# Sliding-window attention and gMLP, four layers: the window mask moved from extra contraction rows to a multiply, and the 64-row remainder of the input projections run as pairs of half-height array tiles

## The chip, the core and the metric

The kernel runs on one core of a Trainium2 chip. The metric is the device time of one execution in microseconds. Three runs of the kernel before took 1401.13, 1403.95 and 1405.71 us; the median is 1403.95 us.

The engines are named as the profile names them: PE is the matrix engine, PEld its weight loads, DVE the vector engine, ACT the scalar engine, POOL the GpSimd engine, and SP the engine that issues most DMAs. SPq, ACTq and POOLq are their DMA queues.

## The reference

The input x has 2048 rows of 576 columns. Four layers run in the order A, B, A, B, and each adds its result to x. Both A layers use the same weights, and so do both B layers.

```
A:  xn = layernorm(x);  q, k, v = xn @ wqkv            (32 heads of 18 columns)
    logits[s, w] = q[s] . k[s - 2w] / sqrt(18),  w = 0..7   (-1e9 where s - 2w < 0)
    x = x + (softmax(logits) @ v) @ wo
B:  xn = layernorm(x);  z = gelu(xn @ w_in)             (576 -> 4608 = 2 x 2304)
    z1 = z[:, :2304];  z2 = layernorm(z[:, 2304:])
    g  = w_sp @ z2 + b_sp                               (w_sp is 2048 x 2048)
    x  = x + (z1 * g) @ w_out
```

A query sees eight keys: its own position and every second one before it.

## The kernel before

All contractions over the 576 columns use the transposed, normalised input `xnT`, a tile of 128 partitions by 5 chunks by 2064 columns. Four chunks are full; the fifth holds 64 columns of x and 64 rows of zeros, which come from zeroed columns 576 to 639 of the LayerNorm output buffers `ln_xn` (four of them, in rotation). A LayerNorm tile is normalised on ACT or POOL (L229, L233) and moved into `xnT` by a transposing DMA on the SP queue (L238).

**Layer A.** `PG` (L469) projects q and k for groups of seven heads and 512 positions: five matmuls of 512 columns into PSUM, then a copy to a staging tile `stg` (L475 on DVE, L477 on ACT, in turn), and, once a staging tile is complete, one DMA for each head into the tile `QK`, where a head has 18 of 32 partitions. Twelve such groups form the prologue, the others are spread over the attention steps. `VW` (L427) makes v. Then come 38 steps, two for each of 19 tiles of 112 queries. In step s, `L_mm` (L546) computes 16 heads' logits as 16 matmuls of 32 rows, four of them in the four row groups of the array; `EXP` (L562 in the late steps, in two halves; L565 in the early ones) takes the exponent on ACT into one of two buffers `P_sb`; `PV` (L588) multiplies by v into the one PSUM tile `O_ps`; `NORM` (L605, L606, on DVE) divides by the sum. A few steps later `TAIL_B` projects with wo (L630), adds x (L632, DVE), and takes LayerNorm statistics for the next layer (L211, DVE), and `TAIL_B2` normalises on POOL (L233). Late steps, which have no `PG` left, carry two dummy matmuls each (L574).

The window is enforced inside `L_mm`: partitions 18 to 31 of each head hold 14 extra rows, for q and for k, whose product is zero inside the window and a large negative number outside it. `build_window_rows` (L120 to L173) makes one period of these rows with small POOL and DVE operations in layer 0 and sends it to DRAM; `fill_window_rows` copies them into `QK`, 16 DMAs of about 225 KB on the SP queue, once in each A layer:

```
        for j in range(4):
            for a in range(2):
                self.dma(QK[32 * j + DH:32 * j + 32, a, :, x0:x1],
                         self.winD[a, :, None, x0:x1].to_broadcast([MR, 8, x1 - x0]), eng=self.nc.sync)
```

In layer 0 these DMAs are issued in the middle of the LayerNorm transposes, in layer 2 at the layer's start.

**Layer B, phase 1** (`p1_main`, 16 row tiles): 2304 columns of z2 as five units (four of 512 columns, one of 256), five matmuls for each (L859); gelu on ACT (L863); sums of squares on DVE (L866) and ACT; a reciprocal root on POOL (L882); the normalised z2 is written by DVE (L895, six slices) and POOL (L892, three slices). Two buffers `zp` hold the gelu output.

**Layer B, phase 2:** 18 times, 20 matmuls of 512 columns for z1 (L943: four column blocks, five chunks) and 64 matmuls for the spatial product (L951). ACT applies gelu (L946), DVE combines (L955, L956). **Phase 3** projects with w_out (L988).

The tile framework orders each engine's instructions by priority. `L_mm` has a raised priority; the rest of a step follows the order of emission.

Of the kernel before, what the change touches and what calls it, by code (L numbers as in the profile page):

```python
# [10 lines left out]
ACT = mybir.ActivationFunctionType  # L11
# [8 lines left out]
P = 128  # L20
# [9 lines left out]
MR = 32 - DH  # L30
WB = 1024.0
# [32 lines left out]
class K:  # L64
# [24 lines left out]
    def setup(self):  # L89
# [10 lines left out]
        nc.vector.memset(self.eps_t[:], EPS)  # L100
        self.xnT = c.tile([P, 5, cfg.XW], bf16, name="xnT")
        nc.gpsimd.memset(self.xnT[:, :, 0:PADL], 0.0)

        self.late_setup = []
# [11 lines left out]
        for b in self.xn_bufs:  # L116
            nc.gpsimd.memset(b[:, D:640], 0.0)
        self.deferred = []

    def build_window_rows(self):  # L120

        nc, c = self.nc, self.consts
        R = c.tile([P, 2, MR, 16], bf16, name="win_rows")
        n = c.tile([P, 3], i32, name="win_n")
        g = c.tile([P, 3], i32, name="win_g")  # L130
        bits = c.tile([P, 5, 3], i32, name="win_bits")
        vf = c.tile([P, 5, 3], f32, name="win_vf")
        uu = c.tile([P, 4, 2], f32, name="win_uu")
        two = c.tile([1, PADL], bf16, name="win_two")
        half = WB / 2
        nc.gpsimd.iota(n[:], pattern=[[1, 3]], base=15, channel_multiplier=1)
        nc.gpsimd.memset(R[:, 0, 0:8, :], half)
        nc.gpsimd.affine_select(out=R[:, 0, 0:8, :], in_=R[:, 0, 0:8, :], compare_op=ALU.is_ge, fill=-half,
                                base=1, pattern=[[2, 8], [-1, 16]], channel_multiplier=0)
        nc.gpsimd.memset(R[:, 1, 0:8, :], 0.0)  # L140
        for off in (2, 3):
            nc.gpsimd.affine_select(out=R[:, 1, 0:8, :], in_=R[:, 1, 0:8, :], compare_op=ALU.not_equal, fill=-1.0,
                                    base=-off, pattern=[[-2, 8], [1, 16]], channel_multiplier=0)
        nc.gpsimd.memset(R[:, 1, 7, 0:2], 1.0)
        for a, v in ((0, half), (1, 1.0)):
            row = R[:, a, 12, :].rearrange("p (f e) -> p f e", e=2)
            nc.gpsimd.memset(row[:, :, 0:1], v)
            nc.gpsimd.memset(row[:, :, 1:2], -v)
        nc.gpsimd.memset(R[:, 0, 13, :], -2.5 * WB)
        nc.gpsimd.memset(R[:, 1, 13, :], 1.0)  # L150
        nc.gpsimd.memset(two[:], 2.0)
        nc.vector.tensor_scalar(out=n[:], in0=n[:], scalar1=15, scalar2=None, op0=ALU.bitwise_and)
        nc.vector.tensor_scalar(out=g[:], in0=n[:], scalar1=1, scalar2=None, op0=ALU.logical_shift_right)
        nc.vector.tensor_tensor(out=g[:], in0=g[:], in1=n[:], op=ALU.bitwise_xor)
        for i in range(4):
            nc.vector.tensor_scalar(out=bits[:, i, :], in0=g[:], scalar1=i, scalar2=1,
                                    op0=ALU.logical_shift_right, op1=ALU.bitwise_and)
        nc.vector.tensor_scalar(out=bits[:, 4, :], in0=n[:], scalar1=1, scalar2=None, op0=ALU.bitwise_and)
        nc.vector.tensor_scalar(out=vf[:], in0=bits[:], scalar1=-2.0, scalar2=1.0, op0=ALU.mult, op1=ALU.add)
        nc.vector.tensor_scalar_mul(out=R[:, :, 0:8, :], in0=R[:, :, 0:8, :], scalar1=vf[:, 4, 1:2])  # L160
        nc.vector.tensor_tensor(out=uu[:], in0=vf[:, 0:4, 0:2], in1=vf[:, 0:4, 1:3], op=ALU.add)
        nc.vector.tensor_scalar_mul(out=R[:, 0, 8:12, :], in0=vf[:, 0:4, 1:2].to_broadcast([P, 4, 16]), scalar1=half)
        nc.vector.tensor_scalar_mul(out=R[:, 1, 8:12, 0:2], in0=uu[:, :, 0:1].to_broadcast([P, 4, 2]), scalar1=0.5)
        nc.vector.tensor_scalar_mul(out=R[:, 1, 8:12, 2:16], in0=uu[:, :, 1:2].to_broadcast([P, 4, 14]), scalar1=0.5)
        one = self.dram.tile([2 * MR, 256], bf16, name="win_period")
        self.winD = self.dram.tile([2, MR, self.cfg.XW], bf16, name="win_all")
        wd = self.winD[:].rearrange("a r x -> (a r) x")
        self.dma(one[:].rearrange("q (p f) -> p q f", f=16), R[0:16].rearrange("p a r f -> p (a r) f"), eng=nc.gpsimd)
        S = self.cfg.S
        self.dma(wd[:, 0:S].rearrange("q (k y) -> q k y", y=256), one[:, None, :].to_broadcast([2 * MR, S // 256, 256]),  # L170
                 eng=nc.gpsimd)
        self.dma(wd[:, S:S + PADL], one[:, 0:PADL], eng=nc.gpsimd)
        self.dma(wd[2 * MR - 1:2 * MR, 0:PADL], two[:], eng=nc.gpsimd)  # L173

    def fill_window_rows(self, QK, x0, x1):
        for j in range(4):
            for a in range(2):
                self.dma(QK[32 * j + DH:32 * j + 32, a, :, x0:x1],
                         self.winD[a, :, None, x0:x1].to_broadcast([MR, 8, x1 - x0]), eng=self.nc.sync)

# [43 lines left out]
    def ln_xn(self, x_t, nrows, mv, rstd, nmr, eng="act"):  # L224
        nc = self.nc
        xn = self.xn_bufs[self.xn_rr % len(self.xn_bufs)]
        self.xn_rr += 1
        if eng == "act":
            nc.scalar.activation(out=xn[:nrows, 0:D], in_=x_t[:nrows, :], func=ACT.Identity,  # L229
                                 scale=rstd[:nrows, 0:1], bias=nmr[:nrows, 0:1])  # L230
        else:
            e = nc.gpsimd if eng == "pool" else nc.vector
            e.tensor_scalar(out=xn[:nrows, 0:D], in0=x_t[:nrows, :], scalar1=mv[:nrows, 0:1],  # L233
                            scalar2=rstd[:nrows, 0:1], op0=ALU.subtract, op1=ALU.mult)
        return xn
# [72 lines left out]
    def layer_A(self, li):  # L308
# [63 lines left out]
        def pad_setup():  # L372
            nc.gpsimd.memset(QK[:, :, :, 0:PADL], 0.0)
            if li == 0:
                self.build_window_rows()
            xc = PADL + CBS[0][1]
            self.fill_window_rows(QK, 0, xc)
            self.fill_window_rows(QK, xc, XW)
# [41 lines left out]
        def VW(t, hh):  # L420
            def f():
# [9 lines left out]
                if hh == 0:  # L431
                    nc.vector.tensor_copy(out=dst, in_=src)
                else:
                    nc.scalar.copy(out=dst, in_=src)
# [14 lines left out]
        def PG(d, qk, cc, use_L=False, in_steps=False):  # L449
            def f():  # L450
# [22 lines left out]
                use_dve = (self.evac_rr % 2 == 0)  # L473
# [63 lines left out]
        def L_mm(s):  # L537
# [5 lines left out]
            for (ftl, j) in order:  # L543
# [3 lines left out]
                                 lhsT=kT[32 * j:32 * j + 32, g, QT * t:QT * t + nk],  # L547
                                 rhs=qT[32 * j:32 * j + 32, g, QT * t + PADL:QT * t + PADL + nq],
# [19 lines left out]
        def JUNK(n):  # L568
# [7 lines left out]
            return f  # L576

# [188 lines left out]
        for s in range(NSTEP):  # L766
            with pr(cfg.prio2):
                EXP(s)
            if s + 1 < NSTEP:
                with pr(cfg.prio):  # L770
                    L_mm(s + 1)
# [23 lines left out]
    def layer_B(self, li):  # L795
# [19 lines left out]
        nc.vector.memset(win2b[64:128, 4 - NPF, :].bitcast(i32), 0)  # L815
        for c in range(NPF, 5):
            kc = 128 if c < 4 else 64
            self.dma(win2b[:kc, c - NPF, :], self.B_w_in[c * P:c * P + kc, Fh:2 * Fh], eng=(nc.sync, nc.scalar)[c % 2])

# [17 lines left out]
        def p1_main(i):  # L837
# [16 lines left out]
            if i == 0:  # L854
                order = [(u, c) for c in range(NPF) for u in units] + [(u, c) for u in units for c in range(NPF, 5)]
            else:
                order = [(u, c) for u in units for c in range(5)]
            for ((ci, c0, sub, w), c) in order:
                nc.tensor.matmul(pzvs[ci][:, sub * 512:sub * 512 + w], lhsT=self.xnT[:, c, PADL + i * P:PADL + (i + 1) * P],  # L859
                                 rhs=win2(c)[:, c0 + sub * 512:c0 + sub * 512 + w],  # L860
                                 start=(c == 0), stop=(c == 4))
# [66 lines left out]
        for jj in range(NB):  # L928
            w1 = p2.tile([P, 5, 256], bf16, name="w1")
            nc.gpsimd.memset(w1[64:128, 4, :], 0.0)  # L930
# [5 lines left out]
            for sub in range(2):  # L936
                z1T = p2.tile([P, S], bf16, name="z1T")
                for q2 in range(0, NQ, 2):
                    nq2 = min(2, NQ - q2)
                    pz1 = self.H_tile("pz1")  # L940
                    for qq in range(nq2):
                        for c in range(5):
                            nc.tensor.matmul(pz1[:, qq, :], lhsT=w1[:, c, sub * P:(sub + 1) * P],  # L943
                                             rhs=self.xnT[:, c, PADL + (q2 + qq) * 512:PADL + (q2 + qq + 1) * 512],
                                             start=(c == 0), stop=(c == 4))
                    nc.scalar.activation(out=z1T[:, q2 * 512:(q2 + nq2) * 512],  # L946
                                         in_=pz1[:, 0:nq2, :].rearrange("p a b -> p (a b)"), func=ACT.Gelu_apprx_tanh)
# [154 lines left out]
```

## Time and profile before

| | |
|---|---|
| profiled execution | 1403.95 us |
| its span | 1401.9 us |
| PE busy | 1251.2 us (89%) |
| DVE busy | 575.4 us (41%) |
| ACT busy | 369.3 us (26%) |
| POOL busy | 343.8 us (25%) |

The profile covers the span from the first instruction to the last; the execution's own time is 2.05 us longer. In the timeline, layer 0 fills the first 220 us or so, layer 1 runs to about 725 us, layer 2 to about 905 us, and layer 3 to the end. Busy shares are averages over all of these; each stage has to be read by itself.

### The profile page before, as it was taken

The page shows a single profiled execution, that of the slowest core. Times are in us where ns is not written, and L with a number is a line of the kernel's source. Part 1 is how long each engine was busy: PE and PEld are TensorE (multiplying, and loading weights), DVE is VectorE, ACT ScalarE, POOL GpSimd, SP SyncE. Part 2 cuts the span into 40 slices and gives each one's busy share as a digit, 9 for nine tenths or more (in the row PEclk, how much of TensorE's full clock was granted, in tenths as well). Part 3 has the DMA queues.
Part 4 walks back from the last instruction along what each step waited for, and adds up shares of the span by engine and source line. Part 5 has one row for each costly group of instructions (what it writes and reads, how often), then busy time and mean ns, then how long its engine had stood idle before and what let it go on. Part 6 is the DMA issues. An engine that isn't in the chain of part 4 may idle for free.

```text
span 1401.9 us, 21432 instructions
## 1 busy us (share of the span) xinstructions
PE 1251.2 (89%) x8656; PEld 659.7 (47%) x8656; DVE 575.4 (41%) x1378; ACT 369.3 (26%) x557; POOL 343.8 (25%) x495
## 2 busy tenths in 40 slices
PE   1089997998999999998994799799999999999997
PEld 0045663443444444444762356444444444444475
DVE  4035674883332332332541367578533332332221
ACT  2045562661111111110221567276310101111000
POOL 7043554881000000001231154568400000000011
PEclk9999999999999999998998899999999999999999
DMA  8954757802000000005759476691200000000132
GB/s 235 111 100 101 139 129 159 165 10 82 9 9 10 9 9 9 1 0 187 192 136 118 98 163 152 143 207 36 75 5 9 9 9 9 9 9 1 64 115 64
DMA packets 184303, 108.56 MB, mean 77 GB/s; under 512 B 138824, under 2 KB 162776, under 8 KB 184204
## 3 DMA queue, kind: packets, MB, share of 16 engines
q1 hardware_dynamic: 174240, 91.55, 30.5%
q0 software_dynamic: 3600, 7.09, 2.2%
q10 hardware_dynamic: 6364, 8.55, 2.2%
q8 instruction: 68, 1.11, 0.3%
q14 instruction: 31, 0.25, 0.1%
HBM read 48.67 MB, written 16.65 MB: 47 GB/s over the span
## 4 chain that ended last, share of the span: by engine, by line
PE 63%; DVE 10%; POOL 9%; DMA 8%; issue 6%; ACT 2%; SPq 1%; ACTq 0%; POOLq 0%
PE pg L951 34%; PE pz L943 11%; PE po L988 10%; POOL ln_xn L233 5%; PE pp L469 4%; DVE z_junkD L866 4%; DVE z2b L895 4%; DMA QK<-stg 2%; DMA QK<-win_all 2%; POOL ln_rstd L216 2%; POOL z_rstd L882 1%; ACT P_sb L565 1%; PE pv L427 1%; DMA wout_b<-in_B_w_out_dram 1%; DMA xnT<-ln_xn 1%
## 5 line engine op out<-in xcount | busy, mean ns | idle before, releaser
L951 PE MATMUL pg<-W_sb,z2b 128*128 128x512 bf16 x2304 | 504.0, 379 | 1.9 <-DVE z2b L895 1.9
L951 PEld LDWEIGHTS <-z2b 128*128 128x128 bf16 x2304 | 225.2, 98 | 273.7 <-DVE z2b L895 2.4
L955 DVE TENSOR_TENSOR g_tmp<-pg,bsp 128x512 f32<-128x512 f32 x144 | 99.4, 692 | 435.6 <-PE pg L951 424.0
L946 ACT ACTIVATE z1T<-pz 128x1024 bf16<-128x1024 f32 x72 | 73.7, 1023 | 555.6 <-PE pz L943 555.3
L469 PE MATMUL pp<-xnT,wqk_sb 128*128 128x512 bf16 x400 | 100.9, 395 | 72.9 <-DMA xnT<-ln_xn 67.7
L943 PE MATMUL pz<-xnT,w 128*128 128x512 bf16 x720 | 162.1, 379 | 3.9 <-DMA w<-in_B_w_in_dram 3.7
L988 PEld LDWEIGHTS <-uT 128*128 128x128 bf16 x1152 | 114.3, 99 | 43.0 <-issue 11.0
L988 PE MATMUL po<-wout_b,uT 128*128 128x288 bf16 x864 | 116.2, 291 | 9.2 <-DMA wout_b<-in_B_w_out_dram 9.1
L859 PEld LDWEIGHTS <-xnT 128*128 128x128 bf16 x800 | 78.8, 99 | 93.8 <-issue 12.8
L930 POOL MEMSET w<- 64x256 bf16 x18 | 5.4, 306 | 465.7 <-PE pz L943 465.6
L943 PEld LDWEIGHTS <-w 128*128 128x128 bf16 x720 | 70.2, 98 | 89.8 <-DMA w<-in_B_w_in_dram 5.5
L859 PE MATMUL pz<-win2a,xnT 128*128 128x512 bf16 x384 | 104.4, 382 | 4.8 <-ACT zp L863 3.4
L956 DVE TENSOR_TENSOR uT<-g_tmp,z1T 128x512 bf16<-128x512 f32 x144 | 99.5, 692 | 14.3 <-ACT z1T L946 4.7
L892 POOL TENSOR_SCALAR z2b<-zp,z_rstd,z_nmr 128x256 bf16<-128x256 bf16 x96 | 102.0, 1072 | 3.6 <-POOL z_nmr L884 0.7
L469 PEld LDWEIGHTS <-wqk_sb 128*128 128x128 bf16 x400 | 37.1, 100 | 115.7 <-issue 81.4
L233 POOL TENSOR_SCALAR ln_xn<-x_new,ln_mv,ln_rstd 112x576 bf16<-112x576 f32 (+1 forms) x38 | 87.0, 2290 | 3.8
L562 ACT ACTIVATE P_sb<-L_ps 128x896 bf16<-128x896 f32 (+1 forms) x88 | 74.1, 870 | 43.8 <-PE L_ps L546 22.3
L859 PE MATMUL pz<-win2b,xnT 128*128 128x512 bf16 x256 | 76.6, 384 | 4.2 <-DMA win2b<-in_B_w_in_dram 4.2
L863 ACT ACTIVATE zp<-pz 128x1024 bf16<-128x1024 f32 x64 | 64.9, 1019 | 45.2 <-POOL z2b L892 37.6
L216 POOL TENSOR_TENSOR ln_rstd<-ln_rstd,neg_half 112x1 f32<-112x1 f32 (+2 forms) x70 | 39.1, 559 | 149.0 <-DVE ln_rstd L215 148.1
L630 PE MATMUL pw<-wo_sb,oT 128*128 128x288 bf16 x380 | 59.2, 301 | 16.4 <-DMA oT<-o_t 16.4
L996 DVE TENSOR_TENSOR x_new<-po,xo 128x288 f32<-128x288 f32 x64 | 28.8, 456 | 103.5 <-PE po L988 103.5
(94 smaller groups left out, 1045.8 us busy)
## 6 DMA issues: line engine op xcount, KB each, us to landing
xo<-xres SPq DMA_DIRECT2D x32, 288.0 KB
xres<-x_new SPq DMA_DIRECT2D x36, 252.0 KB
w<-in_B_w_in_dram SPq DMA_DIRECT2D x72, 64.0 KB
xres<-x_new SPq DMA_DIRECT2D x16, 288.0 KB
xo<-xres SPq DMA_DIRECT2D x18, 252.0 KB
QK<-stg POOLq DMA_DIRECT2D x52, 72.0 KB, 4.6
QK<-win_all SPq DMA_DIRECT2D x16, 227.5 KB
QK<-win_all SPq DMA_DIRECT2D x16, 224.0 KB
```

The source lines that it names most:

```text
L216: nc.gpsimd.tensor_tensor(out=rstd[:nrows, :], in0=rstd[:nrows, :], in1=self.neg_half[:nrows, :], op=ALU.pow)
L233: e.tensor_scalar(out=xn[:nrows, 0:D], in0=x_t[:nrows, :], scalar1=mv[:nrows, 0:1], scalar2=rstd[:nrows, 0:1], op0=ALU.subtract, op1=ALU.mult)
L469: nc.tensor.matmul(pp[:, :], lhsT=wqk_sb[:, c, wc0:wc0 + P], rhs=self.xnT[:, c, col0:col0 + 512], start=(c == 0), stop=(c == 4))
L562: nc.scalar.activation(out=P_sb[:nk, 2 * hh:2 * hh + 2, :, 0:nq], in_=Lv[:nk, 2 * hh:2 * hh + 2, :, 0:nq], func=ACT.Exp, scale=float(scale))
L859: nc.tensor.matmul(pzvs[ci][:, sub * 512:sub * 512 + w], lhsT=self.xnT[:, c, PADL + i * P:PADL + (i + 1) * P], rhs=win2(c)[:, c0 + sub * 5 ...
L892: nc.gpsimd.tensor_scalar(out=z2b[b][:, i, :], in0=zp[:, b * 256:(b + 1) * 256], scalar1=rstd[:, 0:1], scalar2=nmr[:, 0:1], op0=ALU.mult, ...
L943: nc.tensor.matmul(pz1[:, qq, :], lhsT=w1[:, c, sub * P:(sub + 1) * P], rhs=self.xnT[:, c, PADL + (q2 + qq) * 512:PADL + (q2 + qq + 1) * 512],
L946: nc.scalar.activation(out=z1T[:, q2 * 512:(q2 + nq2) * 512], in_=pz1[:, 0:nq2, :].rearrange("p a b -> p (a b)"), func=ACT.Gelu_apprx_tanh)
L951: nc.tensor.matmul(pg[:, :], lhsT=z2b[jj][:, i, sub * P:(sub + 1) * P], rhs=W_sb[:, i, q * 512:(q + 1) * 512], start=(i == 0), stop=(i == ...
L955: nc.vector.tensor_tensor(out=tmp[:], in0=pg[:, :], in1=bsp[:, q * 512:(q + 1) * 512], op=ALU.add)
L956: nc.vector.tensor_tensor(out=u[:, sub, q * 512:(q + 1) * 512], in0=tmp[:], in1=z1T[:, q * 512:(q + 1) * 512], op=ALU.mult)
L988: nc.tensor.matmul(acc[hh], lhsT=uT[j // 2][:, j % 2, i * P:(i + 1) * P], rhs=wout_j(j)[:, hh * 288:(hh + 1) * 288], start=(j == 0), stop= ...
```

## The change

Two things change together.

The extra contraction rows go, with all that builds and copies them. `L_mm` contracts 18 rows instead of 32. In each step, between `EXP` and `PV`, DVE multiplies the 16 heads' exponents by a 0/1 mask tile, one instruction on 128 partitions by 16 by 112 bf16 elements. The mask tiles are made in layer 0 by POOL. The copies out of PSUM are shared out differently: DVE takes every third `stg` copy instead of every second, and every sixth v copy instead of every second; ACT takes the others.

The fifth chunk of `xnT` holds its 64 columns twice, once in each half of the partitions: every LayerNorm tile gets a second copy of 64 columns on the same engine. The weight tiles of both B projections get their last 64 rows twice too, by one more DMA, in place of a memset. The last contraction of each block is then a matmul of 64 rows, and consecutive blocks use opposite halves of the array. In layer B phase 1 the order of matmuls changes with it, for the first row tile too, which before began with the three chunks that are prefetched.

```diff
@@ MASK, new, called after EXP(s) and ahead of L_mm(s + 1)
+            Pv = P_sb[:].rearrange("p a b c -> p (a b) c")
+            nc.vector.tensor_tensor(out=Pv[:nk, :, 0:nq], in0=Pv[:nk, :, 0:nq],
+                                    in1=m[:nk, None, 0:nq].to_broadcast([nk, 16, nq]), op=ALU.mult)
@@ L_mm
-                                 lhsT=kT[32 * j:32 * j + 32, g, QT * t:QT * t + nk],
+                                 lhsT=kT[32 * j:32 * j + DH, g, QT * t:QT * t + nk],
...
@@ pad_setup
             nc.gpsimd.memset(QK[:, :, :, 0:PADL], 0.0)
-            if li == 0:
-                self.build_window_rows()
-            xc = PADL + CBS[0][1]
-            self.fill_window_rows(QK, 0, xc)
-            self.fill_window_rows(QK, xc, XW)
@@ VW and PG, copies out of PSUM
-                if hh == 0:
+                if hh == 0 and t % 3 == 0:
...
-                use_dve = (self.evac_rr % 2 == 0)
+                use_dve = (self.evac_rr % 3 == 0)
@@ ln_xn (and the same with e.tensor_copy on POOL or DVE)
+            nc.scalar.copy(out=xn[:nrows, D:640], in_=xn[:nrows, 512:D])
@@ layer_B
-        nc.vector.memset(win2b[64:128, 4 - NPF, :].bitcast(i32), 0)
...
+        self.dma(win2b[64:128, 4 - NPF, :], self.B_w_in[512:576, Fh:2 * Fh], eng=nc.scalar)
@@ p1_main, units 0 to 4
+            nu = len(units)
+            z_full(range(2), range(4))
+            z_half(range(nu))
+            for u in range(2, nu):
...
@@ phase 2, four blocks q
-            nc.gpsimd.memset(w1[64:128, 4, :], 0.0)
+            self.dma(w1[64:128, 4, :], self.B_w_in[512:576, jj * 256:(jj + 1) * 256], eng=nc.sync)
...
+                def z1_half(q, first):
+                    r = 64 * (q % 2)
+                    nc.tensor.matmul(pz1s[q // 2][:, q % 2, :], lhsT=w1[r:r + 64, 4, sub * P:(sub + 1) * P],
+                                     rhs=self.xnT[r:r + 64, 4, PADL + q * 512:PADL + (q + 1) * 512],
+                                     start=first, stop=not first, tile_position=(r, 0))
+                z1_full(0, True)
+                z1_full(1, True)
+                for q in range(NQ):
+                    z1_half(q, q >= 2)
+                z1_full(2, False)
+                z1_full(3, False)
```

`z1_full` holds the four full chunks of a block; `z_full` and `z_half` do the same for phase 1.

## The prediction

> **What bounds the kernel now.** I read the page's slices first, then the chain of waits in order of time, then the timeline where the chain names something other than PE. All numbers are microseconds unless marked.
>
> ```profile
> PE   1089997998999999998994799799999999999997
> ...
> DVE  4035674883332332332541367578533332332221
> ...
> DMA  8954757802000000005759476691200000000132
> ```
>
> ```profile
> 38.29 18.11 DMA QK<-win_all
> ...
> 58.88 13.06 DMA xnT<-ln_xn
> ...
> 247.58 1.79 DVE z2b L895 x6
> 252.59 1.79 DVE z2b L895 x6
> ...
> 335.54 4.32 PE pz L943 x20
> 339.85 13.81 PE pg L951 x64
> ```
>
> Each slice is 35 long. PE is idle in the second slice (the 0) and for a good part of two slices from 736 on (the 4 and the 7), where DMA stands at 9 and 4. The chain says why: in layer 0 it runs through the window-row DMAs and the transposes behind them. In phase 1 of layer B it runs through DVE with a period of 252.59 - 247.58 = 5.01; in phase 2 it is all PE, 4.32 + 13.81 for each of 36 blocks.
>
> ```profile
> 29.76 22.03 SPq L78 DMA_DIRECT2D QK<-win_all  x16
> ...
> 56.41 19.25 SPq L238 DMA_TRANSPOSE xnT<-ln_xn  x6
> ...
> 72.08 4.85 PE L469 MATMUL pp<-xnT,wqk_sb 128*128 128x512 bf16 x15 [42.67 <-DMA xnT<-ln_xn]
> ...
> 730.44 34.02 SPq L78 DMA_DIRECT2D QK<-win_all  x16
> ...
> 764.57 25.66 SPq L78 DMA_DIRECT2D QK<-stg  x16
> ...
> 775.04 0.96 PE L546 MATMUL L_ps<-QK 32*128 32x112 bf16 x6 [19.55 <-DMA QK<-stg]
> ```
>
> These are the SP queue and PE at the start of layers 0 and 2 (start, length; in brackets PE's idle time). In both, 16 window-row DMAs stand in SP's queue, and what PE needs is issued after them.
>
> **The window rows go.** Layer 0: before 29.76 six of the transposes are issued. The next two, which let PE go on, then need no wait; nine of them took 23.45 from 58.88, so 2.6 each. PE resumes at about 30 + 2 x 2.6 + 1 = 36 instead of 72, a gain of 36. But SP's share of the `stg` DMAs stands behind eight of the transposes in the changed queue: 30 + 8 x 2.6 = 51, against 82.4 before: 31. The attention steps need both, so I take 32, and 28 to 38 as bounds. The replacement for `build_window_rows`, ten POOL operations on 128x128 elements, costs what its rows of before do (0.34 each, so some 3), and those go.
>
> Layer 2: the prologue's projections ended at 739.9 unhindered. In layer 0 the first exponent came 9 after that point (86.5 to 95.4), and the late steps 58 later (153.1). So the late steps could start at 739.9 + 9 + 58 = 807, against 833.6: a gain of 26.6. It is less than the stall, because PE did projections early while it waited, and these come back into the steps. Bounds: 18 to 33.
>
> **The mask multiply comes.** 38 DVE instructions in each A layer on 16 x 112 = 1792 elements. No two-input DVE row of before is all-bf16 and plain, so I bound it:
>
> ```profile
> L956 DVE TENSOR_TENSOR uT<-g_tmp,z1T 128x512 bf16<-128x512 f32 x144 | 99.5, 692 | 14.3 <-ACT z1T L946 4.7
> ...
> L866 DVE CUSTOM_DVE_ANT_0 z_junkD<-zp 128x1536 bf16<-128x1536 bf16 x32 | 56.7, 1771 | 17.6 <-ACT zp L863 17.6
> ...
> L160 DVE TENSOR_SCALAR win_rows<-win_rows,win_vf 128x256 bf16<-128x256 bf16 x1 | 0.3, 286 | 0.0
> ```
>
> ```profile
> 833.00:893.00 60.00, 55.36 (x940) 37.87 (x938) 41.13 (x120) 38.79 (x54) 33.11 (x25) 1.00 0.68 158
> ```
>
> The first two give 1.054 ns an element (1079 ns for 1024 more), so 1771 + 256 x 1.054 = 2.04 for a mask. The third, all-bf16, is 286 ns for 256 elements, where one-element operations take 148 (L215): 0.54 ns an element, so 1792 x 0.54 + 0.15 = 1.12. I take 1.1, because its elements are 16-bit on every side, as the mask's are; 2.04 stays for the range. "VectorE: DVE Perf Modes" in the Trainium skill, section "The perf-mode tier table", states 1224 ns for a bf16 tensor_tensor of 2048 elements in SBUF and 2293 at the plain rate; by it a mask would be an estimated 1.09; no run here shows it.
>
> The window is one of the late steps in layer 2 (busy in it: PE, PEld, DVE, ACT, POOL). A tile of two steps takes 5.36 there (late exponents at 849.1, 854.5, 859.8), so 60 is 11.2 tiles and DVE is busy 3.67 in each. Masks add 2 x 1.1, and two thirds of a v copy (0.45) leave: 3.67 + 2.2 - 0.3 = 5.6. DVE becomes the busiest engine. PE, the busiest before, reached 55.36 of 60; at that share DVE needs 5.6 / 0.923 = 6.05. So 0.24 (no idle time) to 0.69 for each of 11 late tiles in two layers; I take 0.55, as an engine without idle time is shown nowhere here: 0.55 x 22 = 12. Low end 0, if the 5.36 hides them; high end, at 2.04, 3.67 + 4.08 - 0.3 = 7.45, that is 2.1 x 22 = 46.
>
> The 16 early steps take 58 / 16 = 3.6 and are PE's. DVE was busy 30.69 in the 58 from 95, 1.9 a step; with 1.1 more and the shifted copies less (0.35) it is at 2.7. It still fits, but `MASK(s)` waits for `EXP(s)`, and behind it in DVE's order stand `NORM(s-1)`, which frees the only `O_ps`, the `stg` copies and the additions of L632, for which PE waits through its three PSUM buffers. No row prices such queueing. Between 0 and the whole 1.1 (35 in all) I take 0.25, near the low end, as a quarter of DVE's step is left to absorb it: 0.25 x 32 = 8. Masks together: 20.
>
> POOL pays too: a z2b slice takes 0.61 beside DVE's one-input slices and 2.12 beside z_junkD, which reads two SBUF inputs (1.77 long).
>
> ```profile
> 248.07 1.22 POOL L892 TENSOR_SCALAR z2b<-zp,z_rstd,z_nmr 128x256 bf16<-128x256 bf16 x2
> ...
> 249.28 2.12 POOL L892 TENSOR_SCALAR z2b<-zp,z_rstd,z_nmr 128x256 bf16<-128x256 bf16 x1
> ...
> 249.29 1.77 DVE L866 CUSTOM_DVE_ANT_0 z_junkD<-zp 128x1536 bf16<-128x1536 bf16 x1
> ```
>
> So a mask holds POOL for nearly its length. POOL's 33.11 / 11.2 = 2.96 a tile, the second copy of 64 columns (0.2, as a memset of that size) and 2 x 1.1 make 5.4: just under DVE's, so I add nothing.
>
> **The half-height pairs.** Phase 2: 16 full matmuls at 216 ns, then two pairs. What a change of the array's tiling costs is seen at `L_mm`:
>
> ```profile
> 98.47 1.02 PE L469 MATMUL pp<-xnT,wqk_sb 128*128 128x512 bf16 x4
> ...
> 99.42 0.38 PE L546 MATMUL L_ps<-QK 32*128 32x112 bf16 x16
> ...
> 99.73 0.61 PE L469 MATMUL pp<-xnT,wqk_sb 128*128 128x512 bf16 x2
> ```
>
> Four matmuls at 216 ns end at 99.33, and `L_mm` starts 0.09 later. Its 16 matmuls of 112 columns (47 ns each at 216 for 512) would take 0.75 in turn; the next full one starts 0.31 later, so they did run four at a time (0.19), and the way back costs up to 0.12. A block saves 4 x 0.216 - 2 x 0.216 = 0.43 and pays 0.21: 0.22 x 36 = 8. "TensorEngine Tiling (Array Packing)", section "Key Properties", speaks against the change: switching the tiling mode drains the engine. The page gives no figure; without the drain it names the saving would be an estimated 15.5, and the rows above decide for 8. Bounds: 0.43 x 36 = 15.5, if switching costs nothing, and, if the pairs run in turn, a loss of 0.21 x 36 = 7.6.
>
> Phase 1: PE needs 20 x 0.216 + 5 x 0.11 = 4.87 in a loop of 5.01 that DVE and POOL close (z2b, z_junkD, sums, z_rstd, z2b). A saving on PE gives nothing. The first row tile loses its 15 matmuls that needed only prefetched weights; PE waited for `win2b` at 230.81 and 232.97 there, and a third `win2b` DMA stands behind the first on ACT's queue. After it lands, 12 full matmuls are left, 2.2, about what was left before. I take +1 a layer (0 to 2.5). Phase 2 starts with six weight DMAs on SP instead of five: +0.5. The LayerNorm's second copy lengthens the end of each A layer by 0.3 on POOL, and a mask lies in its last step: +0.5. Together +4.
>
> **The sum** on the profiled execution's own 1403.95 (span 1401.9 plus 2.05; also the median of the three runs): -32 - 26.6 + 20 - 8 + 4 = -42.6, so **1361**.
>
> **The rivals.**
> - *Slower: the masks lie in series.* If each step waits for its whole mask, because DVE's order puts it ahead of what PE needs, 76 x 1.1 = 84 stands in place of 20: 1425. Without masks the sum is -62.6, so this decides from 62.6 / 76 = 0.82 a step. For it: `O_ps` is single and its `NORM` comes after the mask. Against it: from one exponent's end, mask, `NORM`, `PV` are 1.1 + 0.7 + 0.5, and the exponent that needs it is two steps (5.36) later. Chance 0.10.
> - *The plain rate.* At 2.04 the late steps cost 46 and the early ones, with DVE at 1.9 + 2.04 - 0.35 = 3.6 against PE's 3.6, some 0.5 each (twice the 0.25), 16: 62 instead of 20 gives 1403. For it: L956; against it: L160. Chance 0.10.
> - *The pairs don't pair* (the change doesn't do what it says): +7.6 instead of -8, so 1377. Against it: the 0.31 above. Chance 0.10.
> - *Masks hidden, stalls gone in full:* -36 - 33 + 4 - 8 + 2 = -71, so 1333. For it: DVE idles a third of the late steps. Chance 0.12.
>
> **How the numbers follow.** The forecast keeps 0.58. Its own terms move it by some 20 either way: 1340 to 1385. The range 1332 to 1398 adds the hidden masks and the unpaired halves, and leaves out the serial masks and most of the plain rate, 0.2. A difference under 0.3%, 4.2, can't be told from no change. Faster: 0.58 + 0.10 + 0.12, and 0.04 of the plain rate: 0.84. The same: 0.04. Slower: the serial masks and a little of the plain rate: 0.12.
>
> **What would show it.** Right: no `QK<-win_all` rows, PE's second slice full, the first late step of layer 2 near 807 plus 4 for the early masks of that layer, `L527` (the mask) near 1.1, z1 at 4.1 for each block, phase 1 still at 5.01. Wrong: a late tile over 6.5, a mask of 2, z1 over 4.32, or SP's `stg` DMAs in layer 0 no earlier than 70.

## The result, and the profile after

The changed kernel takes 1343.91 us (median of 4 runs, 1342.94 to 1345.92) against 1403.29 for the kernel before: a ratio of 0.9578, 95% interval 0.9558 to 0.9598. The profiled execution's span is 1341.8.

The page's slices (tenths busy, 40 slices of 33.5) after:

```profile
PE   1999879999999999998999988799999999999997
...
DVE  4367866862332332323434888488333233332221
...
DMA  9438669220000000007652677970200000000232
```

PE's second slice is full (it was 0), and the hole at the start of layer 2 (a 4 and a 7) is gone. Of the dips left, the 8s from 134 and from 770 on are the late steps of the two attention layers, where VectorE now reaches 8; the 7 behind them takes in the change to the next layer.

The timeline of the changed kernel, SP's queue and PE at the start of layers 0 and 2 (start, length; in brackets PE's idle time):

```profile
28.10 14.84 SPq L186 DMA_TRANSPOSE xnT<-ln_xn  x8
43.05 9.06 SPq L76 DMA_DIRECT2D QK<-stg  x10
...
33.56 13.20 PE L412 MATMUL pp<-xnT,wqk_sb 128*128 128x512 bf16 x50 [3.63 <-DMA xnT<-ln_xn]
...
697.48 33.79 SPq L76 DMA_DIRECT2D QK<-stg  x16
...
695.39 9.87 PE L412 MATMUL pp<-xnT,wqk_sb 128*128 128x512 bf16 x45 [0.80 <-ACT stg L420]
```

No `QK<-win_all` row is left. In layer 0 PE stands for 3.63 instead of 42.67, and the `stg` DMAs start at 43.05 instead of 82.4. In layer 2 they are issued from 697.48 (764.57 before), 6 after the layer's first projection (691.2), and the prologue's projections run through.

The new row of the instruction groups, for the masks of full size; then busy times by stretch (PE, PEld, DVE, ACT, POOL, granted clock, DMA share, GB/s) in the late steps of layer 0 and of layer 2, and in three late tiles of layer 0.

```profile
L527 DVE TENSOR_TENSOR P_sb<-P_sb,mask_base 128x1792 bf16<-128x1792 bf16 x72 | 79.5, 1104 | 12.9 <-ACT P_sb L508 12.7
```

```profile
...
121.30:181.10 59.80, 54.43 (x921) 36.72 (x919) 53.24 (x130) 40.62 (x59) 38.94 (x34) 1.00 0.66 123
772.50:835.40 62.90, 54.83 (x921) 36.85 (x920) 53.23 (x129) 40.63 (x59) 38.01 (x33) 1.00 0.73 149
...
149.10:166.56 17.46, 15.76 (x266) 10.76 (x265) 15.49 (x38) 12.01 (x17) 10.42 (x9) 1.00 0.59 119
```

A mask takes 1104 ns, 1.10 us (the four masks of the short last tile take 404 ns). The last line is the steady part: a late tile takes 17.46 / 3 = 5.82, with PE busy for 90% of it and VectorE for 89%. The same view of two late tiles of the kernel before:

```profile
849.10:859.80 10.70, 10.41 (x178) 7.25 (x177) 7.59 (x23) 7.51 (x10) 5.70 (x4) 1.00 0.60 152
```

There a tile was 5.35, PE filled 97% of it, and VectorE 71%. The first late tile of a layer differs from this, between 5.3 and 8.9 in the runs with one mask or none, so the steady tile says more than a stretch does. The stretches, measured from the first exponent, the first late exponent and the last one, and in layer 2 from the first projection (all in us):

| stretch | before | after |
|---|---|---|
| layer 0, start to first exponent | 95.4 | 59.2 |
| layer 0, early steps | 57.7 | 62.1 |
| layer 0, late steps | 60.6 | 59.8 |
| layer 2, first projection to first exponent | 61.8 | 21.3 |
| layer 2, early steps | 46.0 | 60.0 |
| layer 2, late steps | 58.9 | 62.9 |
| phase 2 (first to last pg), layers 1 and 3 | 330.6, 328.3 | 327.0, 324.4 |

In layer 2 the early steps grew from 46.0 to 60.0: the kernel before had done some of their projections while it waited, and ran 677 matmuls in them, against 749 after.

The chain of waits of the changed kernel in order of time, one block of phase 2:

```profile
973.27 1.73 PE pz L914 x8
975.00 0.54 PE pz L920 x4
975.54 1.83 PE pz L914 x8
977.37 13.81 PE pg L935 x64
```

The four half-height matmuls (L920) take 0.54, and z1 takes 4.10 in place of 4.32. In phase 1 a row tile still takes 5.01.

### The profile page after: what moved, and what is told of

It is laid out like the page before. It is cut to its first block, busy times and chain, and to the rows that moved or that the text cites. A ratio compares the mean times of both kernels' runs of the same rounds, so it can differ in the third digit from the quotient of the medians.

```text
span 1341.8 us, 21436 instructions
## 1 busy us (share of the span) xinstructions
PE 1243.5 (93%) x8656; PEld 636.1 (47%) x8656; DVE 614.1 (46%) x1400; ACT 391.4 (29%) x622; POOL 362.6 (27%) x508
## 5 line engine op out<-in xcount | busy, mean ns | idle before, releaser
L76 POOL DMA_DIRECT2D wout_b<-in_B_w_out_dram x14 | 7.6, 548 | 635.1 <-PE pg L935 635.1
L914 PE MATMUL pz<-xnT,w 128*128 128x512 bf16 x576 | 136.9, 380 | 2.6 <-DMA w<-in_B_w_in_dram 2.6
L180 POOL TENSOR_SCALAR ln_xn<-x_new,ln_mv,ln_rstd 112x576 bf16<-112x576 f32 (+1 forms) x38 | 95.7, 2518 | 3.9
L914 PEld LDWEIGHTS <-w 128*128 128x128 bf16 x576 | 53.4, 98 | 77.9 <-issue 17.8
L527 DVE TENSOR_TENSOR P_sb<-P_sb,mask_base 128x1792 bf16<-128x1792 bf16 (+1 forms) x76 | 81.1, 1067 | 12.9 <-ACT P_sb L508 12.7
L162 POOL TENSOR_TENSOR ln_rstd<-ln_rstd,neg_half 112x1 f32<-112x1 f32 (+2 forms) x70 | 42.3, 605 | 134.2 <-DVE ln_rstd L161 131.4
L838 DVE CUSTOM_DVE_ANT_0 z_junkD<-zp 128x1536 bf16<-128x1536 bf16 x32 | 56.8, 1774 | 26.8 <-ACT zp L835 26.8
L582 PE MATMUL pw<-wo_sb,oT 128*128 128x288 bf16 x380 | 58.9, 300 | 10.5 <-DMA oT<-o_t 8.7
L867 DVE TENSOR_SCALAR z2b<-zp,z_mean,z_rstd 128x256 bf16<-128x256 bf16 x192 | 57.4, 370 | 21.6 <-POOL z_rstd L854 21.6
```

Source lines behind the costliest of these rows:

```text
L527: nc.vector.tensor_tensor(out=Pv[:nk, :, 0:nq], in0=Pv[:nk, :, 0:nq], in1=m[:nk, None, 0:nq].to_broadcast([nk, 16, nq]), op=ALU.mult)
L914: nc.tensor.matmul(pz1s[q // 2][:, q % 2, :], lhsT=w1[:, c, sub * P:(sub + 1) * P], rhs=self.xnT[:, c, PADL + q * 512:PADL + (q + 1) * 512 ...
```

## The experiments

My theory after the result: the fills' price was larger than forecast, and the masks' smaller; the pairs are worth their 0.22 a block. The rivals: the masks cost what was forecast and something else saved the rest; the pairs do not overlap; the fills cost by their places in a queue and not by their bytes. All runs below were timed beside the kernel before (1401.56 to 1402.77).

**Without the pairs** (`e1_no_pairs`): both projections, the zero padding and the LayerNorm as in the kernel before; masks as in the change.

```diff
-                nc.tensor.matmul(..., lhsT=w1[r:r + 64, 4, ...], ..., tile_position=(r, 0))
+                for c in range(5):
+                    nc.tensor.matmul(pz1[:, qq, :], lhsT=w1[:, c, ...], ..., start=(c == 0), stop=(c == 4))
```

> The changed kernel with both input projections back at full height (five contraction chunks of 128 rows, the last half zeros, the old order), and without the second copy of the 64 rows; the masks stay. By the prediction's terms the pairs are worth 0.22 us in each of 36 blocks of phase 2 (8 us), and cost 1 us in the first row tile of a layer, some more at phase 2's start and in the LayerNorm: the total should rise by 4 to 8, to 1348-1352, with z1 back at 4.32 and the first row tile of phase 1 faster by 1 to 2 us. Rival: the pairs gain nothing (their two halves run in turn, or the switch eats them): 1344 or less, z1 unchanged.

Measured: 1349.43, ratio 0.9622 (0.9601 to 0.9643), 5.5 above the changed kernel. Phase 2 takes 330.1 and 328.8, so 7.5 more in the two layers. The timeline of this kernel, a whole z1 between two stretches of pg:

```profile
992.40 4.48 PE L896 MATMUL pz<-xnT,w 128*128 128x512 bf16 x20
996.72 13.54 PE L904 MATMUL pg<-W_sb,z2b 128*128 128x512 bf16 x62
```

From 992.40 to 996.72 is 4.32, as expected. Of the 7.5, 2.0 are given back elsewhere: phase 1's first GELU comes 9.8 and 9.5 after its first matmul, and 11.0 and 10.5 in the changed kernel.

**All halves on the same rows** (`e4_same_rows`):

```diff
-                    r = 64 * (q % 2)
+                    r = 0
```

(and so in phase 1).

> The changed kernel with all halves of the 64-row chunk on the same rows of the array, 0 to 63, so that two can't run side by side (the result is the same; the upper copy is made and not read). If the pairs of before ran side by side, z1 now takes two more 512-column slots in each of 36 blocks, 0.43 x 36 = 15.5 us: 1359, z1 4.53, and phase 1 hides its own. Rival: the pairs never overlapped: 1344, z1 as it is, 4.10.

Measured: 1362.36, ratio 0.9714 (0.9691 to 0.9737), 18.5 above the changed kernel. The timeline of this kernel:

```profile
1000.08 1.89 PE L914 MATMUL pz<-xnT,w 128*128 128x512 bf16 x8
1001.90 1.03 PE L920 MATMUL pz<-xnT,w 64*128 64x512 bf16 x4
1002.87 1.90 PE L914 MATMUL pz<-xnT,w 128*128 128x512 bf16 x8
1004.61 5.56 PE L935 MATMUL pg<-W_sb,z2b 128*128 128x512 bf16 x25
```

z1 goes from 1000.08 to 1004.61: 4.53. The pairs do run side by side. And 4.53 against the full height's 4.32, with as many 512-column slots, is the price of leaving the full tiling and coming back: 0.21. "TensorEngine Tiling (Array Packing)" in the Trainium skill, section "Key Properties", says that a change of the tiling mode drains the engine; these two runs fit that and show what the change costs here. Phase 2 gives 13.7 of the 18.5; phase 1, which I expected to hide its own slots, took some 3.6 more.

**Without the masks** (`e2_no_mask`), which leaves the window out of the computation:

```diff
                 EXP(s)
-                MASK(s)
```

> The changed kernel without the 76 mask multiplications (the window is left out of the computation: every key of a tile counts). By the prediction's price the masks cost 20 us (12 in the late steps, 8 in the early ones): 1324. By what the two traces show (late steps -0.8 and +4.0, early +4.4 in layer 0) they cost 3 to 10 us: 1334-1341, with TensorE still busy over 90% of the late steps. In series with the chain of exponentials they would cost 76 x 1.07 = 81: 1263.

Measured: 1334.97, ratio 0.9528 (0.9503 to 0.9552). So the masks cost 8.9, not 20. The late steps of layers 0 and 2 in this kernel:

```profile
117.00:174.80 57.80, 54.01 (x920) 36.95 (x917) 37.73 (x112) 40.70 (x60) 33.49 (x35) 1.00 0.60 129
...
768.00:823.70 55.70, 54.09 (x921) 37.32 (x918) 37.80 (x112) 40.63 (x59) 33.86 (x34) 1.00 0.69 165
```

VectorE has 15 less to do in each, and they are 2.0 and 7.2 shorter (of the 7.2, 3.5 are the first tile, which takes 8.9 with the masks and 5.4 here; it takes 7.7 in both kernels that have neither masks nor pairs, so this part is hardly the masks'); the early steps are 3.3 and 0.1 shorter. The steady late tile is 5.36, as in the kernel before: the masks cost 0.46 of their 2.2 in it. PE's busy time is the same within 1. What the masks add in the late steps is PE's waiting; in the changed kernel, PE's waits in the late steps of layer 2 are (total, times, longest):

```profile
PE O_ps L540 <- DVE ln_rstd L161: 4.3, 10, 0.7
PE pw L582 <- DMA oT<-o_t: 2.9, 2, 2.5
PE junk L517 <- DVE v_ext L375: 0.4, 2, 0.2
```

The first is the wait for `NORM` to free `O_ps`: the profile names the instruction behind `NORM` on VectorE, which ends 0.05 after it (802.64 and 802.59 in one tile). Without masks there is 0.4 of the second in that stretch and none of the others. The second is not the masks' own: the kernel before has 2.9 of it in the same stretch, and the kernel without masks 2.4 in layer 0.

**Each mask twice** (`e3_mask_twice`):

```diff
                 MASK(s)
+                MASK(s)
```

> The changed kernel with each mask multiplication issued twice in a row (the same result, since it holds only 0 and 1): as much work for VectorE as one mask at half the rate. If VectorE is just short of being the bound of the late steps (53 us busy of 60 to 63), 22 to 23 more masks of 1.07 fill the rest and then lengthen them: +16 a layer, with the early steps (41 of 61 busy) hiding theirs or paying a few us: 1376 (1365-1390). In series with the chain: +81, 1425. Hidden beside TensorE altogether: 1344-1350.

Measured: 1418.29, ratio 1.0115 (1.0094 to 1.0137): 1.15% slower than the kernel before, and outside my 1365 to 1390. The second mask costs 74.4, eight times the first. The late steps, of layers 0 and 2, in this kernel:

```profile
123.40:218.20 94.80, 67.62 (x929) 41.80 (x928) 73.45 (x158) 40.62 (x60) 50.97 (x35) 0.83 0.40 85
817.60:909.10 91.50, 67.96 (x926) 41.09 (x924) 72.64 (x156) 40.83 (x59) 49.81 (x34) 0.84 0.50 106
```

They are 35.0 and 28.6 longer, 1.45 for each of 44 steps, though a mask is 1.09 there and VectorE is busy only 73 of 95. The longest of PE's waits in the first of these stretches names what stands in between, and VectorE's own wait for PE is beside it:

```profile
DVE rec L557 <- PE O_ps L540: 21.2, 9, 4.7
...
PE pw L582 <- DMA oT<-o_t: 15.3, 6, 4.9
```

**The same with the tail later** (`e12_twice_tail_later`). The first tile's rows come out changed in this kernel: its transposed outputs lie in one of three buffers, which a later tile refills first. The amount of work is the same.

```diff
-            for (off, fn) in ((2, TAIL_A(t)), (4, TAIL_B(t)), (5, TAIL_B2(t)), (6, TAIL_C(t))):
+            for (off, fn) in ((2, TAIL_A(t)), (6, TAIL_B(t)), (7, TAIL_B2(t)), (8, TAIL_C(t))):
```

> The kernel with two masks a step (1418), with TAIL_B, TAIL_B2 and TAIL_C each two steps later. If the two masks were so dear, 1.5 in each late step for 1.07 of work, because a late NORM makes the transpose of o_t late, on which TensorE stands with PV queued behind, the late steps fall from 93 towards VectorE's 73 busy: 80, so 1390 in all, with a clock back near 1. Rival: the loop exponent, mask, PV, exponent through the two P_sb buffers sets them: 1410-1420 as it was.

Measured: 1391.60, ratio 0.9915 (0.9901 to 0.9929), 26.7 less than with the tail in its place. Its late steps:

```profile
122.00:200.00 78.00, 62.83 (x934) 40.77 (x933) 74.21 (x151) 40.85 (x60) 51.41 (x35) 0.91 0.44 98
799.50:877.50 78.00, 63.75 (x925) 40.62 (x922) 73.07 (x150) 40.75 (x60) 50.11 (x34) 0.87 0.56 118
```

They fall to 78, with VectorE busy 74 of it, and PE doesn't wait for `oT` any more in either of them. So the loop was: VectorE late, `NORM` late, the transpose of `o_t` late, PE standing at `pw` with `PV` queued behind it, and VectorE waiting for `PV`. Off that loop, VectorE's own work is the bound, at 94 to 95% busy. The clock did not come back to 1, as I had expected it to.

**The fills alone.** Two forms of the kernel before, both with `L_mm` on the 18 rows of a head (the window is left out of the computation): without the fills (`e5_before_no_fills`), and with all 16 of them over an eighth of their columns (`e6_before_eighth_fills`).

```diff
-            self.fill_window_rows(QK, 0, xc)
-            self.fill_window_rows(QK, xc, XW)
+            self.fill_window_rows(QK, 0, xc // 8)
+            self.fill_window_rows(QK, xc, xc + (XW - xc) // 8)
```

> The kernel before, without the 16 fills of the window rows in each A layer; its L_mm contracts the 18 rows of a head alone, so the window is left out of the computation. It has no masks and no pairs: what it gains on the kernel before is the fills' price. By the prediction's terms 32 + 26.6 = 58.6: 1343 (bounds 1335-1353). By the changed kernel without masks (1335) and the pairs' 5.5 it should be 1340. If something else than the fills held PE in these stretches: over 1370.

Measured: 1336.79, ratio 0.9532 (0.9505 to 0.9560): the fills cost 66.0. The late steps start at 115.9 instead of 153.1 in layer 0 (37.2 less), and 78.8 after the first projection instead of 107.8 in layer 2 (29.0 less); together 66.2.

> As the last, but with all 16 fills issued in their places, each over an eighth of its columns: the same number of DMAs and of rows in SP's queue, an eighth of the bytes (the window is left out of the computation). If the stall is SP's queue (the time to hand 16 DMAs over, and the wait for the rows to be built), most of it stays: 1380-1395. If it is the bytes, 3.7 MB a layer at the 150 to 250 GB/s of these stretches, most of it goes: 1342-1355.

Measured: 1351.38, ratio 0.9640 (0.9613 to 0.9668): 51.4 of the 66.0 go with seven eighths of the bytes, and 14.6 stay with the 16 DMAs and the eighth that is left. (The rate that I named was not these stretches': the kernel before moved 111 GB/s from 25 to 95 and 103 from 726 to 788.) SP's queue in this kernel:

```profile
29.66 7.48 SPq L78 DMA_DIRECT2D QK<-win_all  x16
...
701.44 7.04 SPq L78 DMA_DIRECT2D QK<-win_all  x16
708.59 31.29 SPq L78 DMA_DIRECT2D QK<-stg  x16
```

The 16 fills take SP 7 instead of 22 and 34: what SP spent on them went mostly with their bytes, not with the handing over. The rows that `L_mm` contracts play no part in this: its 16 matmuls take 0.40 on 32 rows in the kernel before and 0.40 on 18 rows in the changed one.

**The old split of copies** (`e7_old_split`). The diff also moves PSUM copies from VectorE to ACT; here they are back.

```diff
-                if hh == 0 and t % 3 == 0:
+                if hh == 0:
...
-                use_dve = (self.evac_rr % 3 == 0)
+                use_dve = (self.evac_rr % 2 == 0)
```

> The changed kernel with the old split of PSUM copies: every second projection and every first v half on VectorE instead of every third and every third of these. VectorE gets 0.3 more in each of 22 late tiles and about 0.35 in each of 32 early steps. If VectorE's queue is what the masks lengthen, the late steps pay 0.3 to 0.33 a tile (+7) and the early ones a quarter of theirs (+3): 1354 (1350-1362). If TensorE alone sets both stretches: 1344.

Measured: 1339.75, ratio 0.9546 (0.9520 to 0.9571): 4 less than the changed kernel, not 10 more. The intervals overlap, so a gain isn't shown; a loss of that size is excluded. The steady late tile is 6.00, 0.18 more than with the new split (0.3 expected), so the relief does something there; but the first exponent came at 53.7 instead of 59.2. Since that moment lies between 53.0 and 59.2 in the runs without fills that have the new split, and between 51.6 and 57.6 in those with the old one, I take no cause from it.

**The mask behind NORM** (`e8_mask_after_norm`):

```diff
                 EXP(s)
-                MASK(s)
...
                     NORM(s - 1)
+            MASK(s)
```

> The changed kernel with MASK(s) issued behind NORM(s-1), not ahead of it; nothing else. The masks cost 9 us by the run without them. If they cost it because NORM, which frees the single O_ps and feeds the transposes, stands behind a mask in VectorE's order (PE waited 0.3 to 0.7 for it in ten of eleven late tiles), half or more comes back: 1335-1340. Rival: what counts is VectorE's work as such, or the mask that now comes later holds PV: 1344-1352.

Measured: 1344.81, ratio 0.9595 (0.9568 to 0.9622): no change. It decides nothing. VectorE's timeline in its late steps:

```profile
804.58 1.08 DVE L527 TENSOR_TENSOR P_sb<-P_sb,mask_base 128x1792 bf16<-128x1792 bf16 x1
805.58 0.45 DVE L157 BATCH_NORM_STATS2 ln_st<-x_new 112x6 f32<-112x288 f32 x1
805.95 0.24 DVE L557 RECIPROCAL rec<-O_ps 112x16 f32<-112x16 f32 x1
```

The mask still stands ahead of the reciprocal of `NORM`, as it does in the changed kernel (806.30 and 807.66 there), and the steady tile is the same 5.82: the scheduler orders the late steps so either way. What the order of these two is worth stays open here; the two `O_ps` below answer for the buffer.

**Two more, and a version from the parts.** `e9_parts_kept` keeps masks and phase-2 pairs, takes the old split of copies and phase 1's old full-height order, and writes the second copy only where a gMLP layer follows:

```diff
+            if twice:
                 e.tensor_copy(out=xn[:nrows, D:640], in_=xn[:nrows, 512:D])
...
-            z_full(range(2), range(4))
-            z_half(range(nu))
+            order = [(u, c) for u in units for c in range(5)]
```

> The changed kernel with what the runs so far speak for: the old split of PSUM copies (it came out at 1340), phase 1 back at full height with its old order (its first row tile waits for one weight DMA less, about 1.2 a layer; TensorE isn't its bound), and the second copy of the 64 rows only in the LayerNorm that feeds a gMLP layer. Masks and the pairs of phase 2 stay. 1335-1339. If the run of the old split was only scatter: 1340-1344.

Measured: 1335.98, ratio 0.9520 (0.9504 to 0.9537). Its interval lies below the changed kernel's, so it is faster than that too. The first GELU of phase 1 comes 8.4 and 7.8 after the first matmul (11.0 and 10.5 in the change).

`e10_one_junk` is that with `njunk=1` in place of 2.

> As the last, with one filler matmul in a late step in place of two, 0.22 less for TensorE in each of 44 late steps (9.5 in all). If TensorE still sets the late steps, 5 to 9 less than the last run; if VectorE does now, with the masks, no change within 2; if the fillers keep up the granted clock, more, with a clock under 0.97 in the late steps.

Measured: 1331.36, ratio 0.9500 (0.9482 to 0.9519): 4.6 less than the last, but the intervals overlap. The late steps of layer 2:

```profile
761.30:823.70 62.40, 52.15 (x905) 33.92 (x906) 55.57 (x142) 39.21 (x53) 35.48 (x35) 0.99 0.82 154
```

The steady late tile falls from 6.00 to 5.61, so nearly all of the 0.43 taken from PE's two steps comes back, though PE is busy only 52 of 62 and VectorE 56. Neither engine alone is the bound: with one `O_ps`, a part of PE's work and a part of VectorE's follow each other, as the next run bears out. Its clock stays at 0.97 and 0.99 in the late steps.

`e11_two_O` is `e9_parts_kept` with two `O_ps` and two general PSUM buffers in the attention layers:

```diff
-        return self.ps.tile(shape, dt, name=name, tag="O", bufs=1)
+        return self.ps.tile(shape, dt, name=name, tag="O", bufs=2)
```

> As the run with the parts kept, with two O_ps buffers and two general PSUM buffers in place of one and three, in the attention layers. If the masks' remaining cost is TensorE's wait for NORM to free O_ps (4 to 5 a layer in the late steps), it goes: 5 to 8 less. Rival: two general buffers make the projections and the additions wait for their copies: 5 to 30 more, in the early steps above all.

Measured: 1344.27, ratio 0.9588 (0.9569 to 0.9608), 8.3 more than with one. PE's waits in the late steps of layer 0:

```profile
PE O_ps L543 <- DVE P_sb L530: 0.7, 2, 0.5
...
PE O_ps L543 <- DVE ln_rstd L163: 0.2, 1, 0.2
```

Both expectations were right, each in its place: the steady late tile fell from 6.00 to 5.54 and the late steps from 62.3 and 62.8 to 57.6 and 60.0, while the early ones rose from 60.1 and 60.9 to 67.4 and 63.1. Most of what the masks cost a late tile (6.00 against 5.36 without them) is the wait for the single `O_ps`; the general buffer that pays for the second one is worth more in the early steps. All attention steps together lose only 2.0 of the 8.3; phase 1's first GELUs, 3.1 later in the two layers, and phase 2, 2.1 longer, make up most of the rest, and no run here shows why.

## Why the prediction was right, and what was mis-sized

The mechanism held: two stalls went, masks came, pairs gained a little. The range (1332 to 1398) holds 1344, but the forecast of 1361 is 17 above it, and the rival with hidden masks and full stalls, 1333, was nearer. Two terms were off, the fills and the masks, both to the same side:

| term | predicted | measured |
|---|---|---|
| fills, layer 0 | -32 | -37.2 (without fills) |
| fills, layer 2 | -26.6 | -29.0 (without fills) |
| masks | +20 | +8.9 (without masks) |
| pairs, phase 2 | -8 | -7.5 (phase 2 without pairs) |
| phase 1, second copy, phase 2's start | +4 | +2.0 (5.5 in all without pairs, less 7.5) |
| the new split of copies | (in the masks) | +4.2 (old split; not shown apart from zero) |

The measured column adds up to -58.6 (-37.2 - 29.0 + 8.9 - 7.5 + 2.0 + 4.2); the change measured -59.4. Each of these runs is uncertain by about 3, so that the two agree within 1 is in part luck.

- *Fills of layer 0.* The term that was mis-sized is the 2.6 for a transpose. It is a mean of nine rows, and the first of them stood far longer than the others. SP's queue in the kernel before:

```profile
58.88 9.44 SPq L238 DMA_TRANSPOSE xnT<-ln_xn  x1
...
68.42 13.92 SPq L238 DMA_TRANSPOSE xnT<-ln_xn  x8
82.43 7.94 SPq L78 DMA_DIRECT2D QK<-stg  x9
```

  The other eight took 1.74 each. The runs without fills have no such long row at this point, so I put it down to the fills' transfers. In the changed kernel eight took 14.84, 1.85 each, so the `stg` DMAs started at 43, not 51; the 1.74 that the trace of before held would have said 44. PE resumed at 33.56 (36 predicted). The lower of my two gains was 31; it became 39.
- *Fills of layer 2.* The first late step came 81.3 after the first projection in the changed kernel; the prediction's 807 + 4 is 85.2 after it. Right within 4: the 14 + 9 + 58 of layer 0's pattern was 14 + 7 + 60.
- *Masks, late steps.* Right: 0.46 a steady tile for the 0.55 forecast, 5.82 for 5.91, at 1.10 a mask for 1.1. VectorE was busy 5.16 in it, not 5.6 (neighbouring instructions overlap a little: the mask from 804.58 above ends at 805.66, the next instruction starts at 805.58), and for 0.89 of the time, not 0.923: the two errors cancel, which is luck.
- *Masks, early steps.* This is the term of the masks' sum that was mis-sized: of the 8 about 3.4 came, nearly all in layer 0. PE does wait for `O_ps` behind the mask, but by 1.8 in all of layer 0's early steps, and not at all without masks:

```profile
PE O_ps L540 <- DVE P_sb L527: 1.8, 5, 0.5
```

  So "a quarter of the mask" was too much for steps in which PE is busy 91% of the time. The sum also held the new split inside the masks' 20, as a relief; it came out with the other sign (+4.2), though not clear of the scatter.
- *Nothing for POOL* held: it was busy 10.42 in three late tiles, 3.5 each, not the 5.4 of the sum. In the late steps of layer 0 it is busy 38.94 with the masks and 33.49 without, 0.25 for each of 22: a mask seldom holds it for its whole length (last section).
- *The serial rival* was wrong: a mask costs 0.12 a step (8.9 / 76), not 1.1. A second one costs 0.98 (74.4 / 76), past its point of decision of 0.82, but not in its way: the late steps pay 1.45 each, more than the mask's length, and the early ones 0.28 (8.8 / 32). What brings the high price about is an amount of VectorE work, not the place of a single mask.
- *The plain rate.* I priced it at 1403. Two masks, 2.19 of work, cost 1418, so at the plain rate the change would probably have lost, though no run has one mask of that length. The sum missed the transpose and `pw` in the loop.
- *Pairs that don't pair:* excluded by the 4.53 of the halves on the same rows. The 0.43 saved and the 0.21 paid are both measured.

## What to carry to other kernels

Price a stall by removing its bytes and its queue places apart: here 51 of 66 went with the bytes. And look at the rows one by one before their mean is used as a price: of nine, one long row held 9.44 of 23.45. Work added to an engine that is not the bound costs a fraction of its length until that engine fills (here 0.46 of 2.2 a tile), and then more than its length (here 1.45 for 1.09), when its lateness goes through a DMA back to the engine that feeds it: ask on which side of that point the addition ends, and test it by adding the same again. A half-height pair is worth it where TensorE sets the pace, and only if the slots saved outweigh one change of tiling and back.

## What was not expected of the hardware

*VectorE and GpSimd.* The timeline of the changed kernel, two LayerNorms on POOL with the masks beside them:

```profile
143.63 3.21 POOL L180 TENSOR_SCALAR ln_xn<-x_new,ln_mv,ln_rstd 112x576 bf16<-112x576 f32 x1
149.10 2.29 POOL L180 TENSOR_SCALAR ln_xn<-x_new,ln_mv,ln_rstd 112x576 bf16<-112x576 f32 x1
...
143.65 1.03 DVE L527 TENSOR_TENSOR P_sb<-P_sb,mask_base 128x1792 bf16<-128x1792 bf16 x1
149.62 1.25 DVE L527 TENSOR_TENSOR P_sb<-P_sb,mask_base 128x1792 bf16<-128x1792 bf16 x1
```

Where the two begin together, POOL takes 0.92 more than its 2.29, nearly the mask's length. Where POOL is half a microsecond ahead, it keeps its 2.29 and the mask takes 1.25 for 1.08. Both patterns recur all through the late steps, 8 and 11 times. "SBUF — State Buffer" in the Trainium skill, section "SBUF: two separate sides", says that of a VectorE instruction with two SBUF inputs and a GpSimd instruction that reads SBUF, whichever starts first holds the shared port for its whole instruction and the other is blocked. The first pair fits if the mask came first there, which 0.02 in the record can't tell; the second does not, since the mask ran inside POOL's instruction and lost 0.17, not the 1.8 that were left of it.

*The clock.* With two masks a step, PE was busy 68 of 92 to 95 in the late steps, and its granted clock fell to 0.83 and 0.84; with the tail later (63 of 78) it was 0.91 and 0.87, and with one mask (54 of 60) 1.00. So the kernel in which PE waited longer also ran PE's work slower: 68 for what takes 54 at full clock, and 54.43 / 0.83 is 66. The order is rough (0.87 at a busier PE than 0.91), and no run changes PE's waiting alone, so what sets the clock stays open.
